# Copies of decoded weights issued in the first block, and the order of weight sums on the vector engine in the second

## The chip, the cores and the metric

The kernel runs on one core of a Trainium2 chip. The metric is the device time of one execution in microseconds (us). A core has a matrix engine (TensorE, PE in the profile, with PEld for its weight loads), a vector engine (VectorE, DVE), a scalar engine (ScalarE, ACT), GpSimd (POOL) and a queue engine (SyncE, SP). In this kernel all DMAs that the traces list by line are issued by SP, one after the other, and each engine works its instructions off in the order fixed at compile time.

## The reference

The reference is linear attention with an RMS norm, followed by a token mix and a two-layer network with a residual. Shapes: batch 8, 8 heads, 576 tokens, head width 64, so 512 channels; hidden width 2048; rank 32.

```python
kv = einsum('bhsd,bhse->bhde', k, v)
out = einsum('bhsd,bhde->bhse', q, kv)
x = out / sqrt(mean(out * out) + 1e-6) * g_norm      # heads side by side: [8, 576, 512]
u = x + (x^T @ U @ V)^T                              # mix over the tokens, rank 32
y = u + maximum(u @ w_ch1, 0) @ w_ch2                # w_ch1 512x2048, w_ch2 2048x512
```

U, V and the two weight matrices come as 64-bit floating point numbers, read as pairs of 32-bit words; everything else is float32.

## The kernel before

**Precision.** Most matrix products use a fast 32-bit format, float32r. So that the result keeps its accuracy, an operand is split into a high part (a copy rounded to float32r, on ACT) and a low part (the rest, a subtraction on DVE), and a product is three matmuls: high by high, high by low, low by high.

**Blocks.** The 8 x 576 = 4608 tokens are worked through as nine blocks of 512 columns. The first three (j = 0, 1, 2) are multiplied in the standard way: 16 steps f of 128 hidden units, each with 12 matmuls for the first layer (`ffn1`, L461), a ReLU that also splits (`relu`, L468 to L475, ACT then DVE; its output is the tile `hhl`), and 12 matmuls for the second layer (`ffn2`, L477), done one step later. The result of the first layer has a single PSUM bank (`ps_h`), so the next `ffn1` needs the L475 of the step before. The other six blocks are done in pairs as 2x2 matrices of blocks with seven products instead of eight (a Strassen-like scheme). These products need sums and differences of the weights' quarters, and they read the weights, plain ones and sums, again from DRAM, piece by piece.

**Decoding.** Each of the 16 weight slices f arrives as 64-bit numbers (`raw`). `decode_w` (L207) turns it into float32 and splits it into `ws`, kept whole in SBUF for the three standard blocks. That is one ACT operation (L104), four on DVE (L107, L108, L110, L112), an ACT copy (L117) and a DVE subtraction (L118), all on 128x1024 elements. In the first block, step f decodes slice f + 2 (`AHEAD`).

**Copies and sums.** For the later blocks, each decoded slice is copied to DRAM: `to_dram` (L217) issues a 1 MB DMA from `ws` to `wd` (L220); slice 0, whose two halves are separate tiles, takes two. `sums_of_w` (L240) makes the sums for the pair of slices n and n + 8, in two parts. The first, `one`, joins high and low parts again with two adds (L248, 128x512) and makes four sums (L252, 128x256). The second, `two`, splits them (L117 on ACT, L118 on DVE into `wf`) and writes high and low parts to DRAM in two DMAs (L260, `w1s`). Temporaries are tiles `dec`, of which there are two, shared with the decoding. In the kernel before, `copy_of_w` is called inside `one` of the sum of the first weights, so that the copies of slices n and n + 8 are issued with the sum n. Each copy is held by `keep_in_program_order` behind the DMA traced before it.

**The pairs of heads.** For each batch and each of four pairs of heads, the attention for a later block is done in between: `kv_step` (L288, with `tails`, L297 to L299, and L313), `out_step` with norm and split (L317 to L364: L336 to L341 statistics, L348 and L350 the scaling, L364 the last operation of the split), `turn_step` (L367: a transposition on DVE, L376, four DMAs to DRAM, L379, `xt`, and one DMA back, L381, `ut`), `t_step` and `t4_step` (rank-32 product, L397), and `mix_step` (L446: two matmuls into PSUM banks of the pool `ps_p`, two adds L456 on DVE into `ut`, and the split for the block's input, L416 on ACT and L417 on DVE). The pool `ps_p` has three banks, which the out and mix steps share.

**The end of a block.** `finish` (L484) adds the residual for four outputs: L488 on DVE frees the output's PSUM bank and writes a tile `st` (three buffers), L489 on POOL adds the low part, L490 sends it out.

**Order.** Work beside the matmuls is put down at half steps h: h = 32j + 2f and the next one, for step f of block j. `PAIRS` (L40) and `STEPS` (L36 to L38) give the pairs their half steps: those of batch 2, in the second block, start at 33, 39, 45 and 51, with the output 2, the transposition 3, the rank-32 product 5 and the mix 8 half steps later. So a pair's output step falls on the same half step as the mix of the pair before (41, 47, 53). The sums have 35 + 3n and the half step after it (L826 to L828). This is the order in which the program is traced, not yet that of the engines: the scheduler takes on each engine the earliest traced instruction that is ready by its own model of time, so an operation whose inputs are ready early can be moved ahead of work traced before it. `keep_in_program_order` adds one bond: the instruction stays behind the one traced last before it on the same engine. From the second block on, the matmuls are held like this.

Of the kernel before, what the change touches and what calls it, by code (L numbers as in the profile page):

```python
# [10 lines left out]
F32 = mybir.dt.float32  # L11
# [4 lines left out]
ALU = mybir.AluOpType  # L16
# [3 lines left out]
DM, DF, R = 512, 2048, 32  # L20
# [5 lines left out]
NF = DF // P  # L26
# [7 lines left out]
NATIVE = 2  # L34
# [10 lines left out]
HALF = NF // 2  # L45
# [3 lines left out]
FORMS = ["A11", "A12", "S2", "S1", "S3", "S4", "A22"]  # L49
WITH = ["B11", "B21", "T2", "T1", "T3", "B22", "T4"]  # L50
AHEAD = 2
PLAN = dict(pair=(0, 7, 13, 13), kv=(0, 0, 0, 0), out=(2, 0, 0, 6), stats=(2, 3, 3, 6), mul=(2, 3, 3, 6), xs=(11, 11, 10, 10), tr=(11, 11, 11, 14), t=(14, 14, 12, 14), t4=(18, 18, 14, 18), mix=(18, 23, 21, 23), mt=(42, 42, 42, 42), uv=6, v4=11, w0=49, w1=45, w2=38, w3=49, x0=49, warm=12, fill0=4, fill1=3, fill2=1, fill3=2, u2=60)
ENG = dict(kv='aaaaa', xh='aaaaa', xl='vvvvv', t4='avva', te='aaaa', uh='vaaa', v4='aggg', wh='avg', wl='vvv', ab='vav', u='av')
LOADS = ['uv', 'q1', 'w10', 'kv1', 'w11', 'kv2', 'g', 'q2', 'q3', 'kv3', 'w12', 'w20', 'w13', 'w22', 'w23', 'w21', 'kv4', 'q4']
# [6 lines left out]
def build(ctx: ExitStack, tc: tile.TileContext, kv_in, kvt0_in, kvt_in, q_in, uv_in, g_in, w_in, out):  # L61
    nc = tc.nc
# [26 lines left out]
    def mm(*args, **kw):  # L89
        ins = nc.tensor.matmul(*args, **kw)  # L90
        if pinned[0]:
            tc.keep_in_program_order(ins)
# [22 lines left out]
    def split(hi, lo, src, lo_eng):  # L115

        nc.scalar.copy(out=hi, in_=src)  # L117
        lo_eng.tensor_tensor(out=lo, in0=src, in1=hi.bitcast(F32), op=ALU.subtract)  # L118
# [61 lines left out]
    whole = {}  # L180
    wd, w2d = {}, {}
# [14 lines left out]
    def halves(t):  # L196
        return t.rearrange("p (a c) -> p a c", a=2)
# [19 lines left out]

    def to_dram(name, src):
        t = dram.tile(list(src.shape), F32, name=name)
        tc.keep_in_program_order(nc.sync.dma_start(out=t, in_=src.bitcast(F32)))  # L220
        return t

    def copy_of_w(n):

        ws = []
        for k, f in enumerate((n, n + HALF)):
            if f == 0:
                d1, d2 = [to_dram(f"{which}d0", whole[which, 0]) for which in ("w1", "w2")]
                ws.append(whole["w1", 0])
            else:  # L230
                d = to_dram(f"wd{f}", whole[f])
                d1, d2 = d[:, 0:2], d[:, 2:4]
                ws.append(whole[f][:, 0:2])
            w2d[f] = d2
            for i in range(2):
                wd["w1", n, f"A{k + 1}{i + 1}"] = d1[:, i]
                wd["w2", n, f"A{i + 1}{k + 1}"] = d2[:, i]
        return ws

    def sums_of_w(which, n, get):  # L240

        c = DM // 2
        t = {}

        def one():
            t["plain"] = a = dec.tile([P, 2 * DM], F32, name="dec")
            for k, w in enumerate(get()):
                nc.vector.tensor_tensor(out=halves(a[:, k * DM:(k + 1) * DM]), in0=w[:, :, 0].bitcast(F32), in1=w[:, :, 1].bitcast(F32), op=ALU.add)  # L248
            a11, a12, a21, a22 = (a[:, k * c:(k + 1) * c] for k in ((0, 1, 2, 3) if which == "w1" else (0, 2, 1, 3)))
            for o, in0, in1, op in ((a22, a21, a22, ALU.add), (a21, a11, a21, ALU.subtract), (a11, a22, a11, ALU.subtract),  # L250
                                    (a12, a12, a11, ALU.subtract)):
                nc.vector.tensor_tensor(out=o, in0=in0, in1=in1, op=op)  # L252

        def two():
            hi = dec.tile([P, 2 * DM], F32R, name="dec")
            lo = wf.tile([P, 2 * DM], F32R, name="wf")
            split(hi, lo, t["plain"], nc.vector)
            d = dram.tile([P, 4, 2, c], F32, name=f"{which}s{n}")
            for s, part in enumerate((hi, lo)):
                nc.sync.dma_start(out=d[:, :, s], in_=part.bitcast(F32).rearrange("p (a c) -> p a c", a=4))  # L260
            for k, name in enumerate(("S2", "S4", "S3", "S1") if which == "w1" else ("S2", "S3", "S4", "S1")):
                wd[which, n, name] = d[:, k]

        return [one, two]
# [17 lines left out]
    def bank():  # L282
        bank_no[0] += 1
        if startup[0] and bank_no[0] % (7 - NEARLY) >= 3 - NEARLY:
            return ps_y.tile([P, 512], F32, name="y")
        return ps_p.tile([P, 512], F32, name="pp")
# [113 lines left out]
    def split_cols(b, c, part, lo_eng):  # L400

        m = BLK * (b + 1) - S * b
        if part == 0:
            src, lo = ut32[c][:, 0:m], BLK - m
        else:
            src, lo = ut32[c][:, m:S], 0
        n = src.shape[-1]
        if b + part >= NSTD:
            nc.scalar.mul(out=r_of(b + part)[:, c, lo:lo + n], in_=src, mul=g_sb)
            return  # L410
        uh, ul = ut_of(b + part)
        hi, lo = uh[:, c, lo:lo + n], ul[:, c, lo:lo + n]
        if b == 0:
            split(hi, lo, src, lo_eng)
        else:
            nc.scalar.mul(out=hi, in_=src, mul=g_sb)  # L416
            nc.vector.scalar_tensor_tensor(out=lo, in0=src, scalar=g_sb, in1=hi.bitcast(F32),  # L417
                                           op0=ALU.mult, op1=ALU.subtract)

    def keep_warm(p, n):  # L420

        for _ in range(n):
            mm(spare, lhsT=state[0, p]["t4"], rhs=v4[:, 0:MAIN], start=True, stop=True)
# [22 lines left out]
    def mix_step(b, p):  # L446
        t4 = state.pop((b, p))["t4"]
        n = S // 2
        for lo in (0, n):
            if lo and b >= NATIVE + NSTD:  # L450
                mp = ps_h.tile([P, 512], F32, name="h")[:, 0:n]
            else:
                mp = bank()[:, 0:n]
            mm(mp, lhsT=t4, rhs=v4[:, lo:lo + n], start=True, stop=True)
            own = ut32[p][:, lo:lo + n]
            nc.vector.tensor_tensor(out=own, in0=mp, in1=own, op=ALU.add)  # L456
        split_cols(b, p, 0, nc.vector)
        if b >= NSTD and (b - NSTD) % 2 == 0 or b == B - 1:
            split_cols(b, p, 1, nc.vector)
# [8 lines left out]
    def relu(h):  # L468
        t = hp.tile([P, 2, BLK], F32R, name="hhl")
        relu_to(t[:, 0], t[:, 1], h)  # L470
        return t[:, 0], t[:, 1]
# [206 lines left out]
    spare = ps_h.tile([P, BLK], F32, name="h")  # L678
    for _ in range(PLAN["warm"]):
        mm(spare[:, 0:P], lhsT=kvb[0], rhs=kvb[0], start=True, stop=True)  # L680
# [51 lines left out]

    tasks = [(PLAN["uv"], uv_step), (PLAN["v4"], v4_step)]
    for p in range(NPAIR):
        for name, what in (("kv", kv_step), ("out", out_step), ("stats", stats_step), ("mul", mul_step),
                           ("xs", xsplit_step), ("tr", turn_step), ("t", t_step), ("t4", t4_step)):
            tasks.append((PLAN["pair"][p] + PLAN[name][p], lambda what=what, p=p: what(0, p)))
        tasks.append((PLAN["pair"][p] + PLAN["mix"][p], lambda p=p: keep_warm(p, PLAN[f"fill{p}"])))
        tasks.append((PLAN["pair"][p] + PLAN["mix"][p], lambda p=p: mix_first(p)))
        tasks.append((PLAN["pair"][p] + PLAN["mt"][p], lambda p=p: mix_rest(p)))  # L740
    ahead = 1
# [12 lines left out]
    def at(h, what):  # L754
        tasks.setdefault(h, []).append(what)

    def do(h):
        for what in tasks.pop(h, []):
            what()
# [64 lines left out]
        for p, base in enumerate(bases):  # L824
            pair_tasks(b, p, base, STEPS0 if b == 1 else STEPS if b < NATIVE + NSTD else STEPS2)
    for n in range(HALF):  # L826
        for m, what in enumerate(sums_of_w("w1", n, lambda n=n: copy_of_w(n))):
            at(35 + 3 * n + m, what)  # L828
    at(70, lambda: sb_tiles("ring"))
    at(71, lambda: load_upto(4))  # L830
    at(82, lambda: sb_tiles("u"))
# [3 lines left out]
    for j in (5, 7):  # L835
        for i in range(2):
            for k, what in enumerate(forms_of_u(j, i)):
                at(SB_AT[j] - 8 + 4 * i + k // 3, what)
    y_prev = hprev = None
    for j in range(NSTD):  # L840
        pinned[0] = j > 0
        y = None
        for f in range(NF):
            if j == 0:
                while ahead < min(NF, f + 1 + AHEAD):
                    decode_w(ahead)
                    ahead += 1
            if j == 0 and f < NEARLY:
                h = hs[f]
                ffn1(h, f, [3], j)  # L850
            else:
                h = ps_h.tile([P, BLK], F32, name="h")
                ffn1(h, f, range(ND), j)
            hcur = (f, *relu(h))
            do(32 * j + 2 * f)
            if hprev is not None:
                ffn2(y_prev if f == 0 else y, [hprev])
            if f == 0:
                if j > 0:
                    finish(y_prev, j - 1)  # L860
                y = outputs(j)
            do(32 * j + 2 * f + 1)
            hprev = hcur
        y_prev = y

    k = 0
# [29 lines left out]
    for j in range(NSTD, NBLK, 2):  # L896
# [15 lines left out]
        for g in range(HALF // NR):  # L912
# [9 lines left out]
            for n in range(len(FORMS)):  # L922
                for i in range(2):
# [4 lines left out]
                    which = int(FORMS[n] in ("A12", "S1", "S4"))  # L928
# [63 lines left out]
```

## Time and profile before

| | us |
|---|---|
| median of 3 runs | 897.7 (895.02 to 897.96) |
| the profiled execution | 894.29 |
| its span | 892.5 |
| first block (about) | 50 to 155 |
| second block (about) | 155 to 243 |
| PE busy | 859.4 |
| DVE busy | 643.3 |
| ACT busy | 361.1 |

The span is the stretch from the first to the last instruction in the trace; the rest of the execution's time lies around it. An engine's busy time is the union of its instructions. In a row of a timeline stand the start in us from the span's beginning, the duration, the engine, the line of the kernel, the operation, the tiles (written, then read) and how many instructions of the kind are merged; in brackets how long the engine had been idle and what it waited for. A row of waits gives the engine, what it waited for, the sum in us, the number of times and the longest. A row of a group gives the count, the busy time, the mean duration in ns, and the idle time before its instructions. A row of time stretches gives each engine's busy time and number of instructions, the granted share of the matrix engine's clock, the mean busy share of the 16 DMA engines and the GB/s moved.

### The profile page before, as it was taken

Reading aid. Unit: us, or ns where it says so; the run is one execution under the profiler, and the core shown is the slowest. Engines: PE = TensorE matmul, PEld = TensorE weight load, DVE = VectorE, ACT = ScalarE, POOL = GpSimd, SP = SyncE. Lnnn points to the kernel's source line nnn. Section 1 sums busy time; section 2 is a strip of 40 time slices with the busy share of each in tenths; the row PEclk is TensorE's granted clock in tenths of the full one; section 3 lists DMA queues with packets and bytes.
Section 4 is the critical chain, followed back from the end, with each engine's and each line's share of the span. In section 5 each row is a group of like instructions: output and inputs, shape, how many; then the busy total and the mean of one; then the engine's idle time right before and its main releaser. Section 6 shows DMA issues by size and latency. Waiting matters only on the chain.

```text
span 892.5 us, 12229 instructions
## 1 busy us (share of the span) xinstructions
PE 859.4 (96%) x4262; PEld 715.6 (80%) x4262; DVE 643.3 (72%) x1136; ACT 361.1 (40%) x653; POOL 23.9 (3%) x43
## 2 busy tenths in 40 slices
PE   7799999899999999999999999999999999999998
PEld 7678877778888878778878877888788888888886
DVE  5999999876436757895876859578756885663574
ACT  5445543332223443352433335454435444432441
POOL 2000001100020000110000000000000000000000
PEclk9899999999999999999999999999999999999999
DMA  9972127999436543593967866477676677556665
GB/s 339 407 271 72 51 76 244 357 355 368 157 99 177 139 128 108 184 320 124 327 181 255 280 195 218 149 221 223 216 210 207 194 236 238 187 192 202 193 208 166
DMA packets 105517, 189.09 MB, mean 212 GB/s; under 512 B 10480, under 2 KB 44784, under 8 KB 103536
## 3 DMA queue, kind: packets, MB, share of 16 engines
q1 hardware_dynamic: 105456, 188.31, 63.8%
q8 instruction: 34, 0.56, 0.3%
q14 instruction: 27, 0.22, 0.1%
HBM read 137.02 MB, written 51.25 MB: 211 GB/s over the span
## 4 chain that ended last, share of the span: by engine, by line
PE 71%; DVE 19%; DMA 5%; issue 2%; ACT 1%; SPq 1%; DVEq 0%; ACTq 0%
PE y L90 53%; PE h L90 10%; PE pp L90 8%; DMA w2r<-wd 2%; DVE dec L110 1%; DVE dec L252 1%; DVE hhl L475 1%; DVE dec L248 1%; DVE hs L475 1%; DVE dec L112 1%; DMA ringw<-w1s 1%; DVE x L348 1%; DMA w1raw<-w_in 1%; DVE ws L118 1%; DVE ss L336 1%
## 5 line engine op out<-in xcount | busy, mean ns | idle before, releaser
L90 PE MATMUL y<-hhl,ws 128*128 128x512 f32 x540 | 133.0, 392 | 0.0
L90 PE MATMUL h<-uth,ws 128*128 128x512 f32 x360 | 121.9, 400 | 3.7 <-DVE hhl L475 3.4
L90 PEld LDWEIGHTS y<-hhl,ws 128*128 128x128 f32 x540 | 100.0, 188 | 20.3
L90 PE MATMUL y<-hs,w2r 128*128 128x512 f32 x384 | 93.1, 394 | 3.4 <-DVE hs L475 3.4
L90 PE MATMUL y<-entry,ring 128*128 128x512 f32 x384 | 90.3, 390 | 0.0
L90 PEld LDWEIGHTS y<-hs,w2r 128*128 128x128 f32 x384 | 70.5, 188 | 19.9 <-DVE hs L475 6.2
L90 PEld LDWEIGHTS h<-uth,ws 128*128 128x128 f32 x360 | 68.3, 190 | 20.5 <-DVE hhl L475 6.6
L90 PEld LDWEIGHTS y<-entry,ring 128*128 128x128 f32 x384 | 71.8, 188 | 14.7
L90 PE MATMUL y<-uT,ring 128*128 128x512 f32 x324 | 77.1, 390 | 0.0
L90 PE MATMUL y<-uB,ringw 128*128 128x512 f32 x306 | 74.5, 392 | 0.4 <-DVE st L488 0.3
L90 PE MATMUL h<-utl,ws 128*128 128x512 f32 x180 | 70.7, 393 | 0.0
L90 PEld LDWEIGHTS y<-uT,ring 128*128 128x128 f32 x324 | 60.6, 188 | 12.5
L90 PEld LDWEIGHTS y<-uB,ringw 128*128 128x128 f32 x306 | 56.7, 188 | 12.9 <-DVE st L488 1.0
L556 DVE TENSOR_TENSOR h<-y,h 128x512 f32<-128x512 f32 x48 | 32.9, 688 | 45.0 <-PE y L90 43.0
L90 PE MATMUL y<-uT,ringw 128*128 128x512 f32 x234 | 56.7, 391 | 0.6 <-DVE sums L556 0.6
L474 ACT ACTIVATE hhl<-h 128x512 fp32r<-128x512 f32 x47 | 28.0, 597 | 71.5 <-PE h L90 71.3
L475 DVE SCALAR_TENSOR_TENSOR hhl<-h,hhl 128x512 fp32r<-128x512 f32 x47 | 32.3, 687 | 33.0 <-ACT hhl L474 32.7
L90 PEld LDWEIGHTS y<-uT,ringw 128*128 128x128 f32 x234 | 43.6, 188 | 9.8 <-DVE sums L556 1.0
L648 DVE TENSOR_TENSOR entry<-h,entry 128x1024 fp32r<-128x1024 f32 x24 | 29.3, 1221 | 22.3 <-ACT entry L647 22.2
L90 PE MATMUL pp<-kvb,q_sb 128*128 128x128 f32 x280 | 37.8, 281 | 2.0 <-DVE ut L456 2.0
L125 ACT CAST xh<-x 128x640 fp32r<-128x640 f32 x30 | 21.8, 728 | 43.1 <-DVE x L350 41.8
L90 PEld LDWEIGHTS h<-utl,ws 128*128 128x128 f32 x180 | 34.2, 190 | 6.3
(224 smaller groups left out, 1421.6 us busy)
## 6 DMA issues: line engine op xcount, KB each, us to landing
raw<-w_in SPq DMA_DIRECT2D x30, 512.0 KB, 10.2
wd<-ws SPq DMA_DIRECT2D x15, 1024.0 KB, 7.5
kv_sb<-kv_in SPq DMA_DIRECT2D x29, 512.0 KB, 4.4
ring<-wd SPq DMA_DIRECT2D x58, 256.0 KB, 3.7
ringw<-wd SPq DMA_DIRECT2D x54, 256.0 KB, 3.5
ring<-w1s SPq DMA_DIRECT2D x48, 256.0 KB, 3.8
ringw<-w1s SPq DMA_DIRECT2D x48, 256.0 KB, 3.8
out<-st SPq DMA_DIRECT2D x36, 256.0 KB, 3.5
```

The lines of the kernel that those rows point to most:

```text
L90: ins = nc.tensor.matmul(*args, **kw)
L110: nc.vector.scalar_tensor_tensor(out=bits, in0=high, scalar=0xC0000000, in1=bits, op0=ALU.bitwise_and, op1=ALU.bitwise_or)
L112: nc.vector.scalar_tensor_tensor(out=bits, in0=low, scalar=29, in1=bits, op0=ALU.logical_shift_right, op1=ALU.bitwise_or)
L118: lo_eng.tensor_tensor(out=lo, in0=src, in1=hi.bitcast(F32), op=ALU.subtract)
L125: nc.scalar.copy(out=out, in_=in_)
L248: nc.vector.tensor_tensor(out=halves(a[:, k * DM:(k + 1) * DM]), in0=w[:, :, 0].bitcast(F32), in1=w[:, :, 1].bitcast(F32), op=ALU.add)
L252: nc.vector.tensor_tensor(out=o, in0=in0, in1=in1, op=op)
L336: nc.vector.tensor_reduce(out=ss.rearrange("p (i h) -> p i h", h=2), in_=xv, axis=AX.X, op=ALU.add)
L474: nc.scalar.activation(out=hh, in_=h, func=AF.Relu)
L475: nc.vector.scalar_tensor_tensor(out=hl, in0=h, scalar=0.0, in1=hh.bitcast(F32), op0=ALU.max, op1=ALU.subtract)
L556: nc.vector.tensor_tensor(out=out, in0=in0, in1=in1, op=ALU.add)
L648: nc.vector.tensor_tensor(out=lo, in0=src, in1=hi.bitcast(F32), op=ALU.subtract)
```

## The change

Three things change.

First, the copies. `copy_of_w` no longer belongs to the sums: it takes one slice and issues its copy. In the first block it is called from step 4 on (`WD0`), at the earliest one step after the step whose number the slice has: slices 0 and 1 at step 4, then one or two at each step, up to slice 14 at step 15. Slice 15 is copied at half step 33, in the second block. The copies are no longer held behind the DMA traced before them.

Second, the half steps of the sums: 35 + 6 (n // 2) + 2 (n % 2) in place of 35 + 3n, so two sums follow each other closely: 35, 37, 41, 43, 47, 49, 53, 55.

Third, the order on DVE: the first two adds of each sum of the first weights (L248), and the two adds of each mix of batch 2 (L456), are held behind the DVE instruction traced just before them. The pairs' tasks of a half step are traced ahead of the sums': at 41, 47 and 53 first the mix of one pair, then the output step of the next, then the sum.

```diff
+WD0 = 4
...
     def to_dram(name, src):
         t = dram.tile(list(src.shape), F32, name=name)
-        tc.keep_in_program_order(nc.sync.dma_start(out=t, in_=src.bitcast(F32)))
+        nc.sync.dma_start(out=t, in_=src.bitcast(F32))
         return t
...
-    def copy_of_w(n):
-
-        ws = []
-        for k, f in enumerate((n, n + HALF)):
...
-        return ws
+    def copy_of_w(f):
+
+        if f == 0:
+            d1, d2 = [to_dram(f"{which}d0", whole[which, 0]) for which in ("w1", "w2")]
+        else:
+            d = to_dram(f"wd{f}", whole[f])
+            d1, d2 = d[:, 0:2], d[:, 2:4]
...
+    def w1_of(n):
+        return [whole["w1", n] if n == 0 else whole[n][:, 0:2], whole[n + HALF][:, 0:2]]
...
-                nc.vector.tensor_tensor(out=halves(a[:, k * DM:(k + 1) * DM]), in0=w[:, :, 0].bitcast(F32), in1=w[:, :, 1].bitcast(F32), op=ALU.add)
+                ins = nc.vector.tensor_tensor(out=halves(a[:, k * DM:(k + 1) * DM]), in0=w[:, :, 0].bitcast(F32), in1=w[:, :, 1].bitcast(F32), op=ALU.add)
+                if which == "w1":
+                    tc.keep_in_program_order(ins)
...
-            nc.vector.tensor_tensor(out=own, in0=mp, in1=own, op=ALU.add)
+            ins = nc.vector.tensor_tensor(out=own, in0=mp, in1=own, op=ALU.add)
+            if b == NATIVE:
+                tc.keep_in_program_order(ins)
...
-        for m, what in enumerate(sums_of_w("w1", n, lambda n=n: copy_of_w(n))):
-            at(35 + 3 * n + m, what)
+        for m, what in enumerate(sums_of_w("w1", n, lambda n=n: w1_of(n))):
+            at(35 + 6 * (n // 2) + 2 * (n % 2) + m, what)
...
+    copies = {f: [] for f in range(NF)}
+    for n in range(NF - 1):
+        copies[max(n + 1, WD0 + n * (NF - WD0) // NF)].append(n)
+    at(33, lambda: copy_of_w(NF - 1))
...
+            if j == 0 and f >= WD0:
+                for d in copies[f]:
+                    copy_of_w(d)
```

More of the change, by code (lines that the diff above doesn't have):

```diff
@@ L219, in to_dram @@
         t = dram.tile(list(src.shape), F32, name=name)
-        tc.keep_in_program_order(nc.sync.dma_start(out=t, in_=src.bitcast(F32)))
+        nc.sync.dma_start(out=t, in_=src.bitcast(F32))
         return t
-    def copy_of_w(n):
-        ws = []
-        for k, f in enumerate((n, n + HALF)):
[L227 to L237, printed above, removed]
-        return ws
+    def copy_of_w(f):
[4 more added lines that the diff above has]
+            d1, d2 = d[:, 0:2], d[:, 2:4]
+        w2d[f] = d2
+        k, n = f // HALF + 1, f % HALF
+        for i in range(2):
+            wd["w1", n, f"A{k}{i + 1}"] = d1[:, i]
+            wd["w2", n, f"A{i + 1}{k}"] = d2[:, i]
+    def w1_of(n):
+        return [whole["w1", n] if n == 0 else whole[n][:, 0:2], whole[n + HALF][:, 0:2]]
     def sums_of_w(which, n, get):
```

## The prediction

> **What bounds the kernel now.** I read the page first, then the table of time stretches, then who waited for whom on the matrix engine (PE) where the change works, then the timelines of that stretch. The page:
>
> ```profile
> span 892.5 us, 12229 instructions
> ```
> ```profile
> PE 859.4 (96%) x4262; PEld 715.6 (80%) x4262; DVE 643.3 (72%) x1136; ACT 361.1 (40%) x653; POOL 23.9 (3%) x43
> ```
>
> PE is busy 859.4 of 892.5 us: only 33.1 us can be won without taking matmuls away, and the change takes none. So the question is which PE waits lie where weights are copied and summed. The waits of PE from 120 to 240 us (us in total, times, longest):
>
> ```profile
> PE y L90 <- DVE st L488: 2.4, 1, 2.4
> PE pp L90 <- DVE ut L456: 2.0, 2, 1.0
> PE h L90 <- DVE hhl L475: 0.8, 2, 0.5
> PE h L90 <- DVE utl L417: 0.6, 1, 0.6
> PE pp L90 <- DVE xh L364: 0.6, 1, 0.6
> PE h L90 <- ACT uth L416: 0.2, 1, 0.2
> ```
>
> Together 6.6 us, nearly all behind VectorE (DVE). The stretches around them (busy PE, PEld, DVE, ACT, POOL; granted clock; DMA share; GB/s):
>
> ```profile
> 80.00:100.00 20.00, 20.00 (x101) 16.67 (x100) 19.24 (x30) 12.66 (x21) 0.00 (x0) 1.00 0.25 72
> 160.00:180.00 20.00, 18.52 (x89) 15.58 (x90) 16.04 (x35) 7.08 (x15) 1.39 (x1) 0.91 0.90 346
> 180.00:200.00 20.00, 18.41 (x98) 15.27 (x97) 14.90 (x34) 6.91 (x13) 0.00 (x0) 1.00 1.01 377
> 200.00:220.00 20.00, 19.00 (x101) 15.95 (x100) 13.41 (x27) 5.90 (x12) 0.00 (x0) 1.00 1.00 378
> ```
>
> In the first block (80 to 100) DVE is nearly full and the DMA three quarters idle; in the second (160 to 220) the DMA is full and DVE has 4 to 6.6 us in 20 free. What fills the DMA are the copies (from the page's list of DMA issues: count, KB each, median us to landing) and the sums' own output. The copies' landing, by the line L220:
>
> ```profile
> wd<-ws SPq DMA_DIRECT2D x15, 1024.0 KB, 7.5
> ```
> ```profile
> DMA to landing us min/median/max: 5.2/7.4/9.9
> ```
>
> **The change, term A: the wait at the block's end.** L488 adds the first block's four outputs into `st`, which has three buffers, so the fourth add waits until the first output has gone through L489 on POOL and landed in DRAM. DVE and PE:
>
> ```profile
> 151.94 1.88 DVE L488 TENSOR_TENSOR st<-y,uth 128x512 f32<-128x512 f32 x3
> ```
> ```profile
> 160.66 0.68 DVE L488 TENSOR_TENSOR st<-y,uth 128x512 f32<-128x512 f32 x1
> ```
> ```profile
> 161.40 0.97 PE L90 MATMUL y<-hhl,w2s 128*128 128x512 f32 x3 [2.36 <-DVE st L488]
> ```
>
> The time to landing of these outputs from 140 to 170 us, and then the same step at the second block's end, when the DMA is quiet:
>
> ```profile
> DMA to landing us min/median/max: 4.4/4.8/5.7
> ```
> ```profile
> L488 DVE TENSOR_TENSOR st<-y,uth x4: 681/687/692, 260.6 to 265.5; 128x512 f32<-128x512 f32 x4
> ```
> ```profile
> DMA to landing us min/median/max: 2.0/2.0/2.5
> ```
>
> Quiet, the fourth add starts 265.5 - 260.6 = 4.9 us after the first; here it took 160.66 - 151.94 = 8.72. With the copies (these 15, and one more in halves) gone from this stretch and the sums later (term E), I put it at 151.94 + 4.9 = 156.8, plus 0.7 for itself: 157.5. PE asked for the bank at 161.40 - 2.36 = 159.04, so 1.5 us are to spare and the 2.36 go. Behind the wait the granted clock falls:
>
> ```profile
> 63.80:67.20 3.40, 1.48 (x7) 0.90 (x5) 3.35 (x6) 0.00 (x0) 0.00 (x0) 1.00 0.39 86
> 158.90:162.30 3.40, 1.04 (x5) 0.77 (x5) 3.30 (x7) 0.92 (x4) 0.88 (x1) 1.00 1.09 427
> 162.80:166.20 3.40, 3.40 (x13) 2.92 (x12) 3.26 (x8) 1.70 (x3) 0.02 (x1) 0.50 1.01 416
> ```
>
> 3.4 us at 0.50 is 1.7 us of matmul time lost. A stretch with 1.48 us of PE work was not followed by a fall, one with 1.04 was; without the wait the stretch is full, so I book the 1.7 as well. A = -(2.36 + 1.7) = -4.1; bounds -4.1 and 0 (the wait stays). The Trainium skill ("TensorE: Matmul & The Clock Gate", section "Why this matters for your kernels") says the clock falls only after PE gaps of about 3 us, one idle window; by that the 2.36 us gap would not be the cause, the 1.7 would stay and the sum be 1.7 us smaller. The row at 162.80 speaks against it.
>
> **Term B: mix adds ahead of sums.** In the second block a sum ran on DVE just as PE needed the mix's add to free a bank:
>
> ```profile
> 183.34 1.80 DVE L252 TENSOR_TENSOR dec<-dec 128x256 f32<-128x256 f32 x4
> 185.06 0.82 DVE L456 TENSOR_TENSOR ut<-pp,ut 128x288 f32<-128x288 f32 x2
> ```
>
> That is the wait of 1.0, twice. Now a sum's L248 stands behind whatever DVE operation is traced before it: for even sums L364 of the pair just put out, which itself follows the mix of the pair before. The four L252 and the L118 of a sum are not held, so the odd sum's tail can still meet a mix. Of 2.0 I take 1.4; bounds -2.0 and 0.
>
> **Term C: the end of the first block.** Half the sums floated into stretches where DVE had no room:
>
> ```profile
> 140.93 0.34 SPq L381 DMA_DIRECT2D ut<-xt  x1
> ```
> ```profile
> 145.96 1.23 DVE L118 TENSOR_TENSOR wf<-dec 128x1024 fp32r<-128x1024 f32 x1 [0.25 <-ACT dec L117]
> 147.10 0.82 DVE L456 TENSOR_TENSOR ut<-pp,ut 128x288 f32<-128x288 f32 x2
> ```
> ```profile
> DMA to landing us min/median/max: 3.4/3.4/3.4
> ```
>
> The last pair's data landed at 140.93 + 3.4 = 144.3, but the add came at 147.10, behind a sum. Without sums it can go up to 2.8 us earlier, more than the 0.6 + 0.2 that PE waited. The two hhl waits, 0.8 together and at most 0.5, lie ahead of that, among the last decodings; the first of the five sums that have run before the second block's first pair is through (below) falls among them too. Of 0.8 + 0.8 = 1.6 I take 1.2; bounds -1.6 and, for a transfer that comes late, the rival below.
>
> **Term D: xh.** The one wait on L364, 0.6, lies in the second block, with a sum's L252 woven into that pair's chain on DVE. The next even sum is held behind L364; the odd one may still be in the way. I take 0.3; bounds -0.6 and 0.
>
> **Term E: what the second block takes over.** The sums that DVE did from 128 to 173, and the first L364 of the second block's pairs:
>
> ```profile
> L252 DVE TENSOR_TENSOR dec<-dec 128x256 f32<-128x256 f32 x20 | 9.4, 471 | 0.3
> L248 DVE TENSOR_TENSOR dec<-ws 128x512 f32<-128x512 f32 x9 | 5.8, 686 | 0.0
> L118 DVE TENSOR_TENSOR wf<-dec 128x1024 fp32r<-128x1024 f32 x4 | 5.1, 1272 | 0.4 <-ACT dec L117 0.2
> ```
> ```profile
> 173.29 0.28 DVE L364 TENSOR_TENSOR xh<-x,xh 64x128 fp32r<-64x128 f32 x1
> ```
>
> Five of eight sums, 20.3 us, 4.1 each, move behind 173.29, two per pair and so two in about 20 us. The stretch 180 to 200 shows what that is like; it held two (four L248) less one L118 of 1.2:
>
> ```profile
> L248 DVE TENSOR_TENSOR dec<-ws 128x512 f32<-128x512 f32 x4 | 2.6, 686 | 0.0
> ```
>
> 14.90 + 1.2 = 16.1 of 20 us of DVE, so there is room. But the cover is thin: h has one bank, and PE needs L475 soon after each product:
>
> ```profile
> 189.93 0.69 DVE L475 SCALAR_TENSOR_TENSOR hhl<-h,hhl 128x512 fp32r<-128x512 f32 x1
> ```
> ```profile
> 191.38 0.39 PE L90 MATMUL h<-uth,ws 128*128 128x512 f32 x1
> ```
>
> 191.38 - 190.62 leaves 0.76 us. A 1.23 us L118 ahead of L475 costs 0.5 at worst. But 180 to 200 held two sums with no wait on hhl. I take one such hit in all: +0.5; bounds 0 and 12 (the rival below).
>
> **Term F: the copies in the first block.** A 1 MB copy is 2.8 us at 378 GB/s; 16 over the 75 us from 80 to 155 raise the DMA share there from 0.25 to about 0.84 (an estimate from these rows). Only the pairs' loads and the xt and ut transfers share it. One such load and its use:
>
> ```profile
> 73.02 0.35 SPq L150 DMA_DIRECT2D kv_sb<-kv_in  x1
> ```
> ```profile
> 86.15 1.05 PE L90 MATMUL pp<-kv_sb 128*128 128x128 f32 x8
> ```
>
> It is issued 13 us before its use, longer than the 9.9 us that the slowest copy took. SP, which issues them, waits in order behind each copy's decoding; the loads behind it have those 13 us. F = 0; bounds 0 and 4.5 (a rival).
>
> Sum: -4.1 - 1.4 - 1.2 - 0.3 + 0.5 = -6.5 us. The profiled execution took 894.3 (span 892.5), so the like of it would take 887.8. The runs had a median of 897.7, 3.4 above; carried over: 891.2.
>
> **Rivals.** *The wait at 159 stays* (L488 still queued late on DVE, or the outputs issued late on SP, which waits in order): A is 0, and B to E give -2.4: 895.3. For it: DVE is at 3.30 of 3.40 there. Against: the landing of 4.4 to 5.7 us beside 2.0.
>
> *Copies delay the second block's start.* All transfers are on one queue. The last weights are split into `ws` here:
>
> ```profile
> 132.81 1.20 DVE L118 TENSOR_TENSOR ws<-dec,ws 128x1024 fp32r<-128x1024 f32 x1
> ```
>
> Their copies follow at 134, with the last pair's ut read behind them (140.93). If ut lands like the slowest copy, 9.9 instead of 3.4 us, PE waits 6.5 - 2.8 = 3.7 longer, 0.8 of C is not won: -6.5 + 4.5 = -2.0, 895.7. The Trainium skill ("DMA: Bandwidth & Descriptors", section "Queues, rings and completion order") has a ring consumed in order, which speaks for this. No run shown has copies in the first block, so this is open.
>
> *Slower: DVE blocks on its own sums.* L118 waits for the ACT cast L117 of the same sum (the 0.25 at 145.96). The casts (ns min/median/max):
>
> ```profile
> L117 ACT CAST dec<-dec x8: 1042/1046/1060, 135.1 to 206.7; 128x1024 fp32r<-128x1024 f32 x8
> ```
> Where cast and L118 stand together ahead of L475, DVE is held 1.05 + 1.23, less 0.76: 1.5 us of PE each. All eight sums: 12 us, -7.0 + 12 = +5: 902.7. From seven hits on (10.5 - 7.0 = 3.5) the kernel is slower by over 0.3%. Against: the wait for a cast is 0.25 where it is shown, not 1.05, since DVE finds other work; and the second block's stretch with two sums lost PE time on L456 and L364, not on hhl.
>
> *It does not do what it says:* the order chosen at compile time leaves the copies or sums about where they were: 897.7. The line that held the copies is removed and the sums' holds are direct, so this is unlikely.
>
> **How the numbers follow.** Forecast 0.62; wait stays 0.13; late start 0.12; slower 0.09; no effect 0.04. 0.3% is 2.7 us, about what a measurement of this kernel tells from no change: faster is below 895.0. The rivals at 895.3 and 895.7 lie near that edge and give a part to faster. Faster 0.69, same 0.21, slower 0.10. The likeliest case's own range is the terms' bounds, -8.3 to -4, 889.4 to 893.7. The three runs lie 895.02 to 897.96, so I open below by 2 and above to the no-effect case: 887.5 to 898.
>
> **What would show it.** Right: no PE wait on st L488 near 159 and no clock of 0.5 near 163; outputs landing in 2 to 3 us; DMA share about 0.8 in 80 to 140 and under 0.6 in 180 to 220; no L248 before the first L364 of the second block; two L248 pairs per L364 after. Wrong: PE waits on hhl L475 in the second block of more than 2 us in all, a wait on utl or uth of more than 1 us at the second block's start, or a st wait that is still there.

## The result, and the profile after

| | before | after |
|---|---|---|
| median, us | 898.29 (895.02 to 899.71, 6 runs) | 887.91 (887.35 to 891.07, 6 runs) |
| ratio | | 0.9894, 95% interval 0.9872 to 0.9916 |
| the profiled execution, us | 894.29 | 889.25 |

The change makes the kernel 1.1% faster. In the kernel after, later lines have moved on: the copy L220 is L221, the split of a sum (L117, L118) is L118, L119, the sums' L252 is L254, L364 is L366, the split of a block's input (L416, L417) is L418, L419, the mix's add L456 is L458, L475 is L479, and L488, L489, L490 are L492, L493, L494. In the experiments these lines can lie a few numbers off.

The page of the kernel after, span and busy times:

```profile
span 887.5 us, 12240 instructions
```
```profile
PE 860.4 (97%) x4262; PEld 718.6 (81%) x4262; DVE 645.3 (73%) x1136; ACT 361.7 (41%) x653; POOL 22.9 (3%) x43
```

PE does the same 4262 matmuls in almost the same busy time (859.4 before); the span around them is shorter. The waits of PE from 120 to 240 us, kernel after, all there are:

```profile
PE h L91 <- ACT uth L418: 0.7, 1, 0.7
PE h L91 <- DVE utl L419: 0.2, 1, 0.2
PE pp L91 <- ACT kvb L126: 0.2, 1, 0.2
```

6.6 us have become 1.1: st, ut, xh and hhl are all gone. The four outputs at the first block's end, kernel after (by tile, 140 to 170 us):

```profile
L492 DVE TENSOR_TENSOR st<-y,uth x4: 681/686/692, 152.7 to 158.1; 128x512 f32<-128x512 f32 x4
...
DMA to landing us min/median/max: 2.0/2.7/4.1
```

Half of them land within 2.7 us where it was 4.8, the slowest in 4.1, and the fourth add starts 5.4 us after the first where it was 8.7. The time stretches after (PE, PEld, DVE, ACT, POOL busy; clock; DMA share; GB/s):

```profile
60.00:80.00 20.00, 18.01 (x73) 14.43 (x72) 18.26 (x26) 8.23 (x10) 0.00 (x0) 0.91 0.86 352
80.00:100.00 20.00, 20.00 (x105) 16.77 (x104) 18.78 (x23) 11.38 (x18) 0.00 (x0) 1.00 0.61 226
...
160.00:180.00 20.00, 20.00 (x106) 16.86 (x105) 16.14 (x36) 6.55 (x14) 0.14 (x1) 1.00 0.51 153
180.00:200.00 20.00, 20.00 (x108) 16.98 (x107) 17.12 (x36) 6.60 (x14) 0.00 (x0) 1.00 0.58 173
200.00:220.00 20.00, 20.00 (x110) 17.02 (x109) 17.17 (x36) 6.73 (x13) 0.00 (x0) 1.00 0.64 195
```

PE is full from 160 to 220, at full clock. The DMA there is half busy where it was full: the copies sit in the first block now, where the share in 80 to 100 went from 0.25 to 0.61, and PE is full there as before. DVE does 2 us more in 180 to 200 and nobody waits for it. The order on DVE, kernel after:

```profile
167.84 0.28 DVE L366 TENSOR_TENSOR xh<-x,xh 64x128 fp32r<-64x128 f32 x1
168.16 0.69 DVE L248 TENSOR_TENSOR dec<-w1s 128x512 f32<-128x512 f32 x1
```

The first sum starts at 168.16, behind the second block's first L366; before, five had run by then.

**Where the time came from.** The first and second block together, from PE's first matmul of the first block to its first of the third: first the kernel before, then after. By these matmuls the second block begins at 146.3 in the kernel before and at 147.0 after, and ends at 255.1 and 248.6; the table ahead of the prediction, with about 50 to 155 and 155 to 243, has the blocks too coarse.

```profile
40.07:255.10 215.03, 205.87 (x1005) 169.63 (x1006) 173.09 (x301) 83.92 (x146) 6.21 (x4) 0.98 0.59 211
```
```profile
41.74:248.60 206.86, 203.64 (x1006) 169.40 (x1007) 174.91 (x301) 84.00 (x146) 5.13 (x4) 0.98 0.62 216
```

215.03 became 206.86: 8.2 us less. Of this 5.9 is PE's idle time (9.16 to 3.22). The rest is busy time, 2.2, although this execution has a half-clock stretch in the first block that the one before did not have, and lost the one at 162.80: these two cancel. So waits cost more than their idle time, which can be seen at one of them. PE around the first wait for ut in the kernel before, and the same step after:

```profile
183.51 1.05 PE L90 MATMUL pp<-kvb,q_sb 128*128 128x128 f32 x8
185.57 0.49 PE L90 MATMUL pp<-kvb,q_sb 128*128 128x128 f32 x2 [1.00 <-DVE ut L456]
185.81 0.47 PE L90 MATMUL h<-uth,ws 128*128 128x512 f32 x1
```
```profile
180.46 1.28 PE L91 MATMUL pp<-kvb,q_sb 128*128 128x128 f32 x10
181.49 0.47 PE L91 MATMUL h<-uth,ws 128*128 128x512 f32 x1
```

From the first of ten matmuls to the one behind them: 185.81 - 183.51 = 2.30 before, 181.49 - 180.46 = 1.03 after. A wait listed at 1.00 cost 1.27, since matmuls that otherwise overlap stand apart. The gaps between the starts of all matmuls, worked out one by one, show the same at each wait (0.1 to 0.3 on top), and three more stalls of 0.24 to 0.30 in the kernel before that are too short to be listed.

### The profile page after: what moved, and what is told of

Same layout as the page of the kernel before. It is cut to its first block, busy times and chain, and to the rows that moved or that the text cites. A ratio compares the mean times of both kernels' runs of the same rounds, so it can differ in the third digit from the quotient of the medians.

```text
span 887.5 us, 12240 instructions
## 1 busy us (share of the span) xinstructions
PE 860.4 (97%) x4262; PEld 718.6 (81%) x4262; DVE 645.3 (73%) x1136; ACT 361.7 (41%) x653; POOL 22.9 (3%) x43
## 4 chain that ended last, share of the span: by engine, by line
PE 83%; DVE 10%; DMA 3%; ACT 2%; issue 2%; SPq 0%; DVEq 0%; ACTq 0%
PE y L91 60%; PE h L91 14%; PE pp L91 10%; DMA w2r<-wd 2%; DVE hs L479 1%; DMA kvq<-kv_in 1%; DVE sums L560 1%; DVE dec L248 1%; DVE dec L254 1%; DVE dec L111 1%; DVE ss L338 0%; DVE x L350 0%; DVE ut L458 0%; ACT dec L118 0%; DVE uB L515 0%
## 5 line engine op out<-in xcount | busy, mean ns | idle before, releaser
L91 PEld LDWEIGHTS y<-uT,ring 128*128 128x128 f32 x324 | 60.6, 188 | 12.5
L479 DVE SCALAR_TENSOR_TENSOR hhl<-h,hhl 128x512 fp32r<-128x512 f32 x47 | 32.2, 685 | 19.5 <-ACT hhl L478 19.2
L338 DVE TENSOR_REDUCE ss<-x 128x10 f32<-128x640 f32 x32 | 26.2, 818 | 14.7 <-ACT x L329 14.6
```

The costliest lines, as they stand in the source:

```text
L338: nc.vector.tensor_reduce(out=ss.rearrange("p (i h) -> p i h", h=2), in_=xv, axis=AX.X, op=ALU.add)
L479: nc.vector.scalar_tensor_tensor(out=hl, in0=h, scalar=0.0, in1=hh.bitcast(F32), op0=ALU.max, op1=ALU.subtract)
```

## The experiments

Each is compared with the kernel before on the same chip (median 896.65 us in 29 runs for the first four, 897.05 in 14 for the others). The theory was that of the prediction: copies beside the outputs cost A, sums beside the mix and the decodings cost B to D. Its rivals: the order alone is enough, or only the st buffer matters.

**The copies alone** (copies as in the change; sums at their old half steps, no holds on DVE):

```diff
-        tc.keep_in_program_order(nc.sync.dma_start(out=t, in_=src.bitcast(F32)))
+        nc.sync.dma_start(out=t, in_=src.bitcast(F32))
...
+            if j == 0 and f >= WD0:
+                for d in copies[f]:
+                    copy_of_w(d)
```

> Only the copies are moved into the first block and freed; sums and mix adds as in the kernel before (half steps 35 + 3n, nothing held on the vector engine). My theory (the wait at the first block's end comes from the outputs' slow landing beside the copies; the rest comes from the sums): landing of the first block's outputs falls from 4.4-5.7 to under 3.5 us, the 2.4 us wait on st and the half clock behind it go, the waits on ut, utl, xh and hhl (4.2 us) stay: about -4 us, 894. Rival, all of it is the sums on the vector engine: 0 to -1 us, 897 to 898. Second rival, all of it is the full DMA: the whole -10, 888.

Measured: 895.4 us (12 runs), ratio 0.9983 [0.9967, 0.9998]: a gain of a third of what was expected. The profiled execution is the slowest of the twelve, 899.04. The outputs landed as they should (by tile, 140 to 175 us):

```profile
L488 DVE TENSOR_TENSOR st<-y,uth x4: 675/678/692, 158.0 to 165.4; 128x512 f32<-128x512 f32 x4
...
DMA to landing us min/median/max: 2.1/2.4/3.0
```

The st wait shrank to 0.3, although the fourth add still comes 7.3 us after the first. The two waits on ut, which were expected to stay, are gone as well. But a new wait took their place. PE's largest wait from 120 to 240, and how it came about on DVE and PE:

```profile
PE h L91 <- DVE hhl L475: 3.7, 2, 3.2
```
```profile
166.49 2.01 DVE L119 TENSOR_TENSOR wf<-dec 128x1024 fp32r<-128x1024 f32 x1 [0.44 <-ACT dec L118]
...
168.43 1.13 DVE L417 SCALAR_TENSOR_TENSOR utl<-ut,g_sb,uth 128x128 fp32r<-128x128 f32 x4
...
169.48 1.28 DVE L248 TENSOR_TENSOR dec<-ws 128x512 f32<-128x512 f32 x2
170.68 0.68 DVE L475 SCALAR_TENSOR_TENSOR hhl<-h,hhl 128x512 fp32r<-128x512 f32 x1
...
171.41 0.79 PE L91 MATMUL h<-uth,ws 128*128 128x512 f32 x1 [3.22 <-DVE hhl L475]
```

The split of one sum (L119, with 0.44 of waiting for its cast) and the adds of the next (L248) stand ahead of the L475 that PE needs, and a half-clock stretch follows at 171.3. This is the mechanism of the slower rival, DVE blocked by its own sums, but at the block's boundary and once. It takes back what A gave.

**The order alone** (the sums' half steps and both holds on DVE; the copies go with their sum and stay held):

```diff
+                ins = nc.vector.tensor_tensor(out=halves(a[:, k * DM:(k + 1) * DM]), in0=w[:, :, 0].bitcast(F32), in1=w[:, :, 1].bitcast(F32), op=ALU.add)
+                if which == "w1":
+                    tc.keep_in_program_order(ins)
...
-            at(35 + 3 * n + m, what)
+            at(35 + 6 * (n // 2) + 2 * (n % 2) + m, what)
```

> Only the sums' new half steps and the two holds on the vector engine; a copy is still issued with its sum and held on the queue, so the copies now come after 168 us and fall into the second block and after. My theory: no copies are left beside the first block's outputs, so that wait goes too, and so do the waits behind the sums; the full DMA in the second block costs little because the mix adds have slack: about -8 to -9 us, 889 to 890. Rival, the copies have to be in the first block because their 44 us of DMA time delays ut, the pairs' loads and the second block's outputs: a new wait on ut or on st near 260 and no more than -4 us, 894 or above.

Measured: 898.23 us (12 runs), ratio 0.9998 [0.9978, 1.0019]. The forecast of 889 to 890 failed, and the rival held. The waits on st, xh, utl and uth are gone here too, but the copies now crowd the second block. The issues on SP and the wait of PE:

```profile
194.64 2.22 SPq L220 DMA_DIRECT2D wd<-ws  x2
...
198.10 1.07 SPq L383 DMA_DIRECT2D ut<-xt  x1
```
```profile
206.00 0.80 PE L90 MATMUL pp<-kvb,q_sb 128*128 128x128 f32 x2 [7.15 <-DVE ut L458]
```

A pair's ut, read back from DRAM, leaves at 198.10 behind two 1 MB copies and lands about 7 us later; PE waits 7.15 us, and the clock is at 0.50 for 6.8 us, from 203.4, within the wait, to 210.2. What the order gains, the copies take back one block later.

**The st buffer alone** (the kernel before, the fourth output of the first block in a tile of its own):

```diff
-            xt = sc.tile([P, 4, NT, 32], F32, name="xt")
+            xt = sc.tile([P, 4, NT, 32], F32, name="xt", tag="xt")
...
-            o = st.tile([P, DM], F32, name="st")
+            if j == 0 and c == ND - 1:
+                o = sc.tile([P, DM], F32, name="st3", tag="xt")
+            else:
+                o = st.tile([P, DM], F32, name="st")
```

> The kernel before, but the fourth output of the first block gets a tile of its own (the slot of xt), so its add need not wait for the first output's landing; copies and sums stay. My theory: the 2.4 us wait on st at 159 us and the half clock at 163 go, nothing else: -4 us, 894. Rival, the fourth add is late because of the sums queued ahead of it: the wait stays at 1 us or more and the gain is under 1.5 us.

Measured: 894.82 us (12 runs), ratio 0.9977 [0.9962, 0.9993]. The wait on st and the half clock behind it are gone, though the outputs land no faster (5.4 us); so it hung on the buffer, as term A says. Whether on its late landing is not shown by this run, since the order on DVE changed too: the four adds stand from 152.7 to 155.8, and the fourth is no longer behind a sum's two adds. But only about 1.8 of A's 4.1 us stay won. PE behind it:

```profile
168.57 0.50 PE L90 MATMUL h<-uth,ws 128*128 128x512 f32 x1 [1.29 <-DVE hhl L475]
...
172.59 0.27 PE L90 MATMUL pp<-xh,u 128*64 128x128 f32 x1 [0.71 <-DVE xh L364]
```

The 2.36 us in which PE stood still were time in which DVE caught up; without them DVE, which still has five sums to do there, is late at the next two places.

**Without the hold on the mix's adds**, and **without the hold on the sums** (the kernel after, one hold taken out each):

```diff
-            ins = nc.vector.tensor_tensor(out=own, in0=mp, in1=own, op=ALU.add)
-            if b == NATIVE:
-                tc.keep_in_program_order(ins)
+            nc.vector.tensor_tensor(out=own, in0=mp, in1=own, op=ALU.add)
```

> The changed kernel without the hold on the mix's adds; sums still held, copies in the first block. My theory: the even sums stand behind the last operation of the output step anyway, and that follows the mix, so the mix's hold is worth little: +0 to +1 us, 888 to 889, with at most 1 us of waits on ut. Rival, the hold on the mix is what removed the 2.0 us of waits on ut: +2 us, 890, and those waits are back.

```diff
-                if which == "w1":
-                    tc.keep_in_program_order(ins)
```

> The changed kernel without the hold on the sums; the mix's adds stay held, the copies stay in the first block. My theory now: the copies and the sums' place each remove one wait and open another, and only together do they pay; with free sums the vector engine is overfull at the end of the first block, as in the run with the copies alone: 5 us or more of waits on hhl between 130 and 180 us, 894 to 896. Rival, the copies' place and the mix's hold suffice: 888.

Measured: without the mix's hold 887.1 us (5 runs), ratio 0.9884 [0.9864, 0.9905], no different from the change; its trace has the operations of DVE, ACT and PE in the very order of the kernel after. Without the sums' hold 895.9 us (10 runs), ratio 0.999 [0.9968, 1.0011]: the whole gain is gone, as forecast (894 to 896). Here the operations of all three engines stand in the very order of the copies alone, and PE's largest wait, 120 to 240, is the same row:

```profile
PE h L91 <- DVE hhl L477: 3.7, 2, 3.2
```

So the hold on the sums is the half of the change that acts on DVE. The new half steps and the mix's hold do nothing by themselves, since this run has them and the copies alone has neither, in the same order. Whether the sums' hold needs the new half steps was not run. The kernel without the mix's hold also tells what the blocks cost when no half-clock stretch falls inside them but the one at their start that both have; its first and second block:

```profile
40.10:245.30 205.20, 201.99 (x1007) 168.16 (x1008) 173.89 (x298) 83.57 (x146) 5.13 (x4) 0.99 0.63 221
```

215.03 - 205.20 = 9.8 us less than before: 5.9 of idle time, 1.7 of half clock, and 2.2 of matmuls that stood apart.

**The copies late** (the kernel after, copies held and issued two each at half steps 60 to 67, around the end of the second block):

```diff
-        nc.sync.dma_start(out=t, in_=src.bitcast(F32))
+        tc.keep_in_program_order(nc.sync.dma_start(out=t, in_=src.bitcast(F32)))
...
-    for n in range(NF - 1):
-        copies[max(n + 1, WD0 + n * (NF - WD0) // NF)].append(n)
-    at(33, lambda: copy_of_w(NF - 1))
+    for n in range(HALF):
+        at(60 + n, lambda n=n: [copy_of_w(n), copy_of_w(n + HALF)])
```

> The changed kernel with the copies taken out of the first block and issued, held in order, at half steps 60 to 67, two at each, so around the end of the second block. My theory: the time up to 230 us is as in the changed kernel (no wait on st at the first block's end), so the first block has no merit of its own; but at the second block's end outputs land in 4 us and more beside the copies and a wait on st of 2 us or more comes up there, or one on ut: 890 to 894. Rival, copies beside the outputs do no harm: 888. Second rival, the copies are harmful wherever the matrix engine is busy: 896.

Measured: 907.12 us (4 runs), ratio 1.0119 [1.0079, 1.0159]; I had expected a gain, and missed by far. The third block starts at 247.7, as early as in the kernel after, and then the second block's outputs meet the copies. POOL, SP, DVE, PE, and the outputs' landing (250 to 290):

```profile
254.07 3.76 POOL L493 TENSOR_TENSOR st<-st,utl 128x512 f32<-128x512 f32 x3 [95.37 <-DVE st L492]
```
```profile
264.01 5.16 SPq L494 DMA_DIRECT2D out<-st  x3
```
```profile
276.65 0.69 DVE L492 TENSOR_TENSOR st<-y,uth 128x512 f32<-128x512 f32 x1 [13.01 <-DMA out<-st]
```
```profile
277.40 1.65 PE L91 MATMUL y<-hhl,w2s 128*128 128x512 f32 x3 [17.11 <-DVE st L492]
```
```profile
DMA to landing us min/median/max: 5.4/10.0/12.5
```

It is term A again at the next block's end, seven times as long. Here DVE itself stands idle for the DMA, 13.01 us. Two things make the first output late: SP, which works in order, issues it at 264.01, some 8.7 us after POOL is done with it, and it then takes 12.5 us to land.

**The copies early but held** (the kernel after, each copy again behind the DMA traced before it):

```diff
-        nc.sync.dma_start(out=t, in_=src.bitcast(F32))
+        tc.keep_in_program_order(nc.sync.dma_start(out=t, in_=src.bitcast(F32)))
```

> The changed kernel with each copy again held behind the transfer traced before it, so that none is issued before step 4 of the first block. Theory: the copies' earliest place is no part of the gain, since nothing near them waits for a transfer: 887 to 889, the share of the DMA lower before 70 us and higher after. Rival, a held copy waits for its decoding and holds loads or the ut transfers behind it: waits on ut or on loads by 150 us, 890 or more.

Measured: 904.26 us (5 runs), ratio 1.0088 [1.0052, 1.0124]; missed too. The copies are called at the same steps as in the change, but leave together. SP, PE, and the outputs' landing (140 to 180):

```profile
136.45 13.53 SPq L221 DMA_DIRECT2D wd<-ws  x12
```
```profile
171.29 1.22 PE L91 MATMUL y<-hhl,w2s 128*128 128x512 f32 x2 [15.18 <-DVE st L492]
```
```profile
DMA to landing us min/median/max: 2.5/13.8/18.8
```

Twelve copies in 13.5 us, right ahead of the outputs; the first of these goes out at 151.63, takes 18.8 us to land, and DVE is idle for it for 15.05 us. What counts is when a copy leaves, not at which step it is called, and the removed hold is what lets it leave early: in the change the first whole slice goes at 52.16 and eight by 86.

**The kernel before, once more:**

> The kernel before, unchanged, for a second look. Theory: the waits of the matrix engine between 45 and 370 us are the same ones to 0.2 us, and what differs from run to run is the number of stretches at half clock, 1.6 to 1.7 us each where the matrix engine is busy; runs lie between 894 and 900. Rival: waits themselves change from run to run.

Measured: 897.54 us. The waits from 120 to 240 are the same six, to 0.1 us. Its first and second block:

```profile
40.50:257.20 216.70, 207.59 (x1006) 170.89 (x1007) 173.26 (x301) 84.38 (x146) 6.21 (x4) 0.98 0.58 209
```

It is 3.3 us longer than the first profile of the same kernel: 1.7 here and 1.5 in the third block, each with one more half-clock stretch (at 67.7 and 327.1). So the first profile of the kernel before met fewer half-clock stretches by chance.

## Why the prediction was right

The direction was right, and so was the core of the mechanism: PE lost time at the first block's end and behind the sums, and the change takes those waits away. The range was met narrowly, and by luck in part: 887.91 lies 0.4 above its lower end, which had been opened by 2 us for the scatter of the runs, and below the 889.4 to 893.7 of the likeliest case. Measured medians differ by 10.4 us, the forecast had 6.5. Three readings behind the terms A, B and C were wrong or half wrong; term by term:

- **A**, the wait for st and the half clock behind it, 4.1: came in full, but slow landing explains only the smaller part of the wait. The predicted start of the fourth add, 156.8, was 158.1, in an execution whose first block began 1.7 us later. In the kernel before, the first output's issue, its landing, and DVE ahead of the fourth add at 160.66:

```profile
154.72 0.40 SPq L490 DMA_DIRECT2D out<-st  x1
```
```profile
DMA to landing us min/median/max: 4.4/4.4/4.4
```
```profile
158.27 1.29 DVE L248 TENSOR_TENSOR dec<-ws 128x512 f32<-128x512 f32 x2
...
160.05 0.69 DVE L475 SCALAR_TENSOR_TENSOR hhl<-h,hhl 128x512 fp32r<-128x512 f32 x1
```

  The output had landed at 154.72 + 4.4 = 159.1, when PE asked for the bank at 159.04. With the add's own 0.7 the landing explains a wait of 0.8 at most; the other 1.5 of the 2.36 us passed while DVE, never idle, did a sum's adds and an L475 that stand ahead of the fourth add. That is a part of the rival's reason (L488 queued late on DVE), though not its outcome. With the copies alone, where an output lands in 2.4, the fourth add comes 7.3 us after the first: of the way from 8.7 to 5.4, moving the copies made 1.4, and the rest came only with the sums away. That outputs which land late can stop PE by themselves is shown by the two kernels with the copies elsewhere: waits of 17.1 and 15.2, with DVE idle for the DMA.
- **B**, the mix, 1.4: both waits went, 2.0 listed and about 2.5 by the starts of the matmuls. The step that named the means was half wrong. The hold on the mix's add orders nothing. And the waits on ut are gone from the two kernels without the sums' hold too; those pay 3.7 on hhl instead. So the hold is not needed for these two waits by themselves; what it buys is that no wait on hhl comes up in their place.
- **C**, the end of the first block, 1.2: the hhl waits went, three of them, 1.1 in all, with two more that were too short to be listed. The second half failed: PE still waits 0.9 for uth and utl (0.8 before), with no sum of weights about. DVE and PE in the kernel after:

```profile
148.32 0.43 PE L91 MATMUL pp<-v,t 128*128 128x288 f32 x2
```
```profile
148.95 0.82 DVE L458 TENSOR_TENSOR ut<-pp,ut 128x288 f32<-128x288 f32 x2
150.51 0.69 DVE L419 SCALAR_TENSOR_TENSOR utl<-ut,g_sb,uth 128x448 fp32r<-128x448 f32 x1 [0.74 <-ACT uth L418]
```

  The last pair's mix has its matmuls at 148.32, after the second block has begun (147.0); in the kernel before they came at 146.00, ahead of its beginning (146.3). This goes with the freed copies, which change the order at compile time: in all four kernels that have them the mix comes 1.5 to 2 us after the block's beginning, and PE waits 0.9 to 1.5 for uth and utl and 0.2 for kvb. In the three with held copies and held sums (the order alone, late, early but held) it comes 0.1 ahead, and none of these waits is there. So without sums that part of C can be had, and the way in which the copies were freed gives it away.
- **D**, xh, 0.3: went in full, 0.6.
- **E**, the sums in the second block, +0.5, bound 12: cost nothing. DVE is at 17.1 of 20 where 16.1 was estimated, and PE has no wait on hhl there. The rival's mechanism exists, as the two kernels without the sums' hold show: one such wait of 3.2 us and its half clock undo the gain. The hold keeps the sums away from the block's boundary, where DVE has no room.
- **F**, the copies in the first block, 0: right as far as the DMA goes, but the 1.1 us of waits named under C come with the copies' freedom, which the sum did not have. The share was 0.61 in 80 to 100, not 0.84, because the copies float forward and begin at 52, in a stretch (60 to 80) that reached 0.86. In 180 to 200 it was 0.58, in 200 to 220 0.64, over the 0.6 that was named as its limit. The rival of a late second block did not come.

What the sum left out is the time that a wait costs beyond its listed idle time: 2.2 us over the two blocks. So the premise that only PE's 33.1 us of idle time can be won does not hold: its busy time fell as well. With the 2.2, the idle time (5.9) and the half clock (1.7) the blocks give 9.8, against 6.5 predicted, and that is within 0.6 of what the medians show. That the profiled executions differ by only 5.0 is chance in the clock: the one after begins the first block 1.7 us later and has half-clock stretches at 69.1 and at 318.3 that the one before has not. Neither sum nor anchor allowed for that, so that the predicted 887.8 came near the profiled run (889.25) is luck: two errors nearly cancel.

Neither half of the change is worth much alone: 0.17% for the copies, nothing that can be told from zero for the order; the buffer alone gave 0.23%. Both together give 1.1%. The prediction added the terms as if they were independent. They are not: each half removes one late thing and lets PE run into the other one, DVE's sums in the one case, the copies in the other. The added terms came near only because both are removed at once.

## What to carry to other kernels

Where two engines or queues are late at the same place, undoing one moves the wait to the other: look up what is late next, and by how much, before a half of a change is judged worthless. Large background copies belong where neither an output with few buffers nor a read that is needed soon shares the queue; check when they leave in the trace, not where the program calls them. Price a wait by the starts of the matmuls around it and by the clock behind it, not by its idle time alone.

## What the runs showed of the hardware

**Half the clock after short waits, but not always.** The same wait of 2.0 us on hhl near 67 stands in the kernel after and in the one without the mix's hold. Stretches of the kernel after, there and in the third block, and of the other:

```profile
65.70:69.10 3.40, 1.41 (x7) 0.83 (x6) 3.35 (x6) 0.00 (x0) 0.00 (x0) 1.00 1.03 431
69.10:72.50 3.40, 3.40 (x8) 2.73 (x9) 3.37 (x4) 2.09 (x2) 0.00 (x0) 0.51 0.78 299
314.90:318.30 3.40, 1.81 (x9) 1.09 (x7) 2.95 (x9) 1.31 (x4) 0.00 (x0) 1.00 0.14 52
318.30:321.70 3.40, 3.40 (x13) 3.11 (x14) 2.48 (x9) 1.78 (x4) 0.00 (x0) 0.50 0.42 94
```
```profile
63.80:67.20 3.40, 1.51 (x7) 0.94 (x5) 3.35 (x6) 0.00 (x0) 0.00 (x0) 1.00 1.02 417
67.20:70.60 3.40, 3.29 (x14) 2.74 (x15) 3.36 (x4) 2.05 (x3) 0.00 (x0) 1.00 1.01 423
```

At 69.10 the clock falls for 3.4 us, in the other kernel, whose engines work in the same order, it does not; at 318.30 it falls after waits of 0.83 and 0.76 us. The two profiles of the kernel before show the same: both have the wait of 2.0 us, and only the second has a fall behind it (at 67.7). The Trainium skill ("TensorE: Matmul & The Clock Gate", section "What's actually happening") has a window of 3.4 us that runs free of the kernel. The traces agree: within each of the ten, the falls lie on one grid of 3.413 us. In the kernel after they come at 11.11, 35.00, 41.83, 69.14 and 318.31, which are 7, 9, 17 and 90 steps after the first. So the windows can be placed where nothing falls, too, and the busy time of PE in each be added up. From 46 us on, in all ten traces, each of the 15 full-clock windows with 1.47 us of PE's busy time or less was followed by a half one. Of the some 2400 with 1.51 or more, only five were, each at one place of the third block, with 1.82 or 1.83 us, as here at 318.31; why is open. The wait near 67 falls into one window in the kernel after (65.72 to 69.14, PE busy 1.42) and reaches over a window's end in the other (63.73 to 67.14, PE busy 1.58). So the same wait acts or not by where it falls in the grid, and that is chance. The advice of the Trainium skill against gaps of over about 3 us ("TensorE: Matmul & The Clock Gate", section "Why this matters for your kernels") is not borne out: a fall came behind a wait of 2.0 us. A stretch costs some 1.7 us where PE is full, and their number differs between executions of one kernel: two of them make up the 3.3 us between the two profiles of the kernel before.

**DVE beside POOL.** In the kernel with the copies alone, the L119 at 166.49 took 2.01 us where the row at 145.96 in the prediction has 1.23. POOL at that time:

```profile
166.13 1.29 POOL L489 TENSOR_TENSOR st<-st,utl 128x512 f32<-128x512 f32 x1 [2.22 <-DVE st L488]
```
The Trainium skill ("SBUF — State Buffer", section "SBUF: two separate sides") says that a DVE operation with two SBUF inputs and GpSimd lock each other out of a shared pair of ports for a whole instruction. The row agrees; 0.8 of that kernel's 3.2 us wait on hhl comes from it by this reading, which no run here tested by itself.
